# A seven-product scheme (Strassen) for the second matrix product of the last two tiles

## The chip, the cores and the metric

The kernel runs on one core of one Trainium2 chip. A core has five engines that run side by side, each through its own list of instructions in order, and that wait for each other through semaphores: TensorE (PE), which multiplies matrices out of SBUF into PSUM; VectorE (DVE) and ScalarE (ACT), which work on SBUF and PSUM; GpSimd (POOL), which works on SBUF and issues transfers; and SyncE (SP), which issues transfers. The metric is the time of the whole program on the device, in microseconds (us), as the median of three runs.

## The reference, cut to what matters

```python
def _attn_ref(q, k, v):                       # q, k, v: 8 x 8 x 576 x 64 (batch, head, position, 64)
    scores = scale * np.matmul(q, k.transpose(0, 1, 3, 2))
    mask = (rel >= 0) & (rel < 64)            # rel: own position less the key's
    scores = np.where(mask, scores, -1e9)
    attn = softmax(scores)                    # over the keys
    return np.matmul(attn, v)

x = attention output, batch and position as 4608 rows, heads side by side as 512 columns
h = x @ w_in                                  # 512 x 2048
g = h * np.cos(h)
return g @ w_out                              # 2048 x 512
```

Each of the 4608 rows of the attention's output goes through two matrix products with a gate between them. `x @ w_in` is the first product, `g @ w_out` the second.

## The kernel before, in words

The 4608 rows are cut into nine tiles of 512 rows (`mt` = 0 to 8). For one tile PE makes the first product as 16 column blocks of 128 (`ff`), each from four matmuls of 512 columns that accumulate in one PSUM bank (`first`, L458). As soon as a block is done ACT takes its sine with a shift (the cosine, `sin`, L597) and DVE multiplies (`gT`, L600, bf16). The 16 blocks of `gT` lie in eight buffers of two. The second product then has four groups of 128 rows (`ms`); each accumulates 16 matmuls of 512 columns, with `gT` as the loaded weights and `w_out_sb` as the moving operand, into one bank (L611). A copy (DVE or ACT, L121) brings the bank to `out_sb`, and SP stores it (`store`, L478). In the last tile the last 128 rows are made in two column parts of 384 and 128 (`last_rows`, L470), so that the last copy and transfer are small.

The attention of batch `b` is made beside the products of earlier tiles: loads of q, k and v by POOL (L166, L172), scores on PE (L289, L311), maximum and mask on DVE (L326), exponent on ACT (L338), reciprocal on DVE (L348), the product with it on POOL (`w`, L355), the turn of `w` by a transfer that SP issues, copies of parts of v on POOL (`spread_v`, L121), and the product with v on PE (`values`, L390), which `put_x` copies into `xT`, the input of the next tile's first product. The last batch, 7, is worked on in tile 6; the value products of tile 8 are made inside the second product of tile 7.

The order on each engine is written out in the program. Tile 0 follows the list `FIRST`. From tile 1 on a plan holds steps with due times in units of which a tile has `T` = 32: `at(time, fn, ...)` enters a step, and `pump(time)`, called after each block of the first product and after each quarter of a group of the second, issues all steps that are due. The due times set only the order of instructions; an engine runs ahead of them where its waits allow.

PSUM has eight banks. Three rotate under one tag (`ps_t`), the other five have names: `O1`, `X0`, `X1`, `S`, `O0`. The first product's blocks go round them in this order (`H_BANKS`), and begin with the blocks 0, 1, 2 (`SKEW` = 3) side by side, in `O1`, `X0`, `X1`. The second product uses `O1` and `O0`. SBUF buffers rotate too: `out_sb` has three, `sin` four.

Of the kernel before, what the change touches and what calls it, by code (L numbers as in the profile page):

```python
# [14 lines left out]
F32 = mybir.dt.float32  # L15
BF16 = mybir.dt.bfloat16
AF = mybir.ActivationFunctionType
ALU = mybir.AluOpType
# [14 lines left out]
Q = 16  # L33
T = 2 * Q
# [3 lines left out]
OUTS = 3  # L38
FILL = (6, 12)
TURNED = {4: 2, 5: 2, 6: 2, 7: 6}  # L40

# [23 lines left out]
def kernel(  # L67
# [9 lines left out]
    nc = tc.nc  # L77
# [3 lines left out]
    d_model = H * D  # L81
    d_ff = moe_w_in.shape[1]
    n_ff = d_ff // 128
    MT = 512
    TU = MT // 64
    n_mt = B * S // MT

    ctx.enter_context(tc.manual_schedule())
    const = ctx.enter_context(tc.tile_pool(name="const", bufs=1))
    ld = ctx.enter_context(tc.tile_pool(name="ld", bufs=2))  # L90
    att = ctx.enter_context(tc.tile_pool(name="att", bufs=3))
    moe = ctx.enter_context(tc.tile_pool(name="moe", bufs=2))
# [6 lines left out]
    w_out_sb = const.tile([128, n_ff, d_model], BF16, name="w_out")  # L99
# [4 lines left out]
    mask16 = const.tile([128, 6, 128], BF16, name="mask16")  # L104

    small = const.tile([128, 1], F32, name="small")

    st = {}

# [5 lines left out]
    half = MT // 2  # L115

    def bank(which, name):
        return ps.tile([128, 512], F32, tag=which, name=name)

    def copy(engine, out, in_):  # L120
        {"a": nc.scalar.copy, "p": nc.gpsimd.tensor_copy}.get(engine, nc.vector.tensor_copy)(out, in_)  # L121
# [20 lines left out]
    def rows_tile(name):  # L142
        return ld.tile([128, NC * H * D], BF16, tag=name, name=name)
# [49 lines left out]
    def transposed(name, b, p):  # L193
# [7 lines left out]
        else:  # L201
            for c in range(TURNED.get(b, 0) if name == "q" else 0, NC):
                nc.tensor.transpose(t_ps[:, NP * c:NP * c + NP], of[:, c, 128 * p:128 * p + 128], ident[:NP, :NP])  # L203
# [9 lines left out]
    def put_q(b, p, engine=None):  # L213
        if b > 1:
            lo = TURNED.get(b, 0) * NP
            copy(engine, qsets[b % 2][:, p, lo:], st.pop(("tq", b, p))[:, lo:])
# [232 lines left out]
    def exp_table():  # L449
        nc.scalar.activation(small, small, AF.Exp, scale=0.0)  # L450
# [4 lines left out]
    def first(mt, ff, ks, start, stop):  # L455
        if start:
            st["h", ff] = bank(H_BANKS[mt == 1][ff], "h_ps")
        nc.tensor.matmul(out=st["h", ff], lhsT=w_in_sb[:, ks, ff * 128:ff * 128 + 128],  # L458
                         rhs=st["xT", mt][:, ks], start=start, stop=stop)

    def skewed(mt, ks, n):
        for ff in range(SKEW):
            first(mt, ff, ks, n == 0, n == PAIRS - 1)

    def last_rows(gT, o_sb):
        ms = MT // 128 - 1
        for which, lo, hi in (("O0", 0, LAST), ("S", LAST, d_model)):
            o_ps = bank(which, "out_ps")[:, lo:hi]
            for ff in range(n_ff):
                nc.tensor.matmul(out=o_ps, lhsT=gT[ff // 2][:, ff % 2, ms * 128:ms * 128 + 128],  # L470
                                 rhs=w_out_sb[:, ff, lo:hi], start=ff == 0, stop=ff == n_ff - 1)
            to = moe.tile([128, MT], F32, tag="sin", name="last_sb", bufs=4)[:, lo:hi] if lo else o_sb[:, 1, lo:hi]
            copy("d" if lo else "a", to, o_ps)
            (nc.sync if lo else nc.scalar).dma_start(out=out[n_mt * MT - 128:n_mt * MT, lo:hi], in_=to)

    def store(o_sb, mt, ms0, e, n):
        r0 = mt * MT + (ms0 + e) * 128
        nc.sync.dma_start(out=out[r0:r0 + n * 128].rearrange("(a p) f -> p a f", p=128), in_=o_sb[:, e:e + n])  # L478

    plan = []  # L480

    def at(time, fn, *args):
        plan.append((time, len(plan), fn, args))

    def pump(time):
        plan.sort(key=lambda x: x[:2])
        while plan and plan[0][0] <= time:
            _, _, fn, args = plan.pop(0)
            fn(*args)
# [20 lines left out]
    for b in range(2, B):  # L510
        t0 = T * (b - 1)
        for c in range(TURNED.get(b, 0)):
            at(t0 - T + (24.3 if b == 4 else 23.4 if c < 2 else 26.4) + 0.01 * c, turn_q, b, c)
        for p in range(PAIRS if TURNED.get(b) != NC else 0):
            t_q = t0 + (2 if b == 2 else 1) + (3.3 if b == 2 else 3.5) * p
# [8 lines left out]
        for c in range(5):  # L524
            at(t0 + (8 if TURNED.get(b) == NC else 0.5) + c, load_v, b, c)
        for half_ in range(2):
# [13 lines left out]
            at(time + (0.2 if p < 2 else 0.2 + 0.1 * p), put_x, mt, p, "a" if p == 2 else None)  # L540


    for i in (2, 1):
        at(T + 4 - 0.1 * i, g_trans, n_listed - i)

# [35 lines left out]
    for mt in range(1, n_mt):  # L581
        base = mt * T
        gT = []
        for ks in range(PAIRS):
            pump(max([base - 1] + [time for time, _, fn, args in plan if fn is put_x and args[:2] == (mt, ks)]))
            skewed(mt, ks, ks)
        for ff in range(n_ff):
            for ks in range(PAIRS):
                if ff >= SKEW:
                    first(mt, ff, ks, ks == 0, ks == PAIRS - 1)  # L590
            h_ps = st.pop(("h", ff))
            sin = moe.tile([128, MT], F32, tag="sin", name="sin", bufs=4)
            if ff % 2 == 0:
                gt = moe.tile([128, 2, MT], BF16, tag="gT", name="gT", bufs=n_ff // 2 + 2)
                gT.append(gt)
            e = ff % 2
            nc.scalar.activation(sin, h_ps, AF.Sin, bias=math.pi / 2.0)  # L597
            if ff == n_ff - 1 and mt < B - 1:
                exp_table()
            nc.vector.tensor_tensor(out=gt[:, e], in0=h_ps, in1=sin, op=ALU.mult)  # L600
            pump(base + ff)
        for ms0 in range(0, MT // 128, 2):
            o_sb = moe.tile([128, 2, d_model], F32, tag="out", name="out_sb", bufs=OUTS)
            o_ps = [bank(which, "out_ps") for which in (("O1",) if mt == n_mt - 1 and ms0 else ("O1", "O0"))]
            for e in range(2):
                ms = ms0 + e
                if mt == n_mt - 1 and ms == MT // 128 - 1:
                    last_rows(gT, o_sb)
                    break
                for ff in range(n_ff):  # L610
                    nc.tensor.matmul(out=o_ps[e], lhsT=gT[ff // 2][:, ff % 2, ms * 128:ms * 128 + 128],  # L611
                                     rhs=w_out_sb[:, ff], start=ff == 0, stop=ff == n_ff - 1)
                    if ff % 4 == 3:
                        if ff == n_ff - 1:
                            copy("a" if e and (mt > 1 or ms0) else "d", o_sb[:, e], o_ps[e])
                            if mt == n_mt - 1:
                                store(o_sb, mt, ms0, e, 1)
                        pump(base + Q + 4 * ms0 + (e * n_ff + ff) // 4)
            if mt < n_mt - 1:
                at(base + T + 0.5 + ms0 / 2, store, o_sb, mt, ms0, 0, 2)  # L620
# [30 lines left out]
```

## Time and profile before

| what | value |
|---|---|
| median of three runs | 306.56 us (305.95 to 306.98) |
| span of the profiled execution | 304.8 us |
| PE busy in it | 293.2 us, 96% |
| DVE, ACT, POOL busy | 217.4, 233.7, 195.8 us |

The profile gives the profiled execution's own time as its span, from the first to the last instruction; the median of the runs is 1.76 us above it, which is what lies around the span. In the profile's lines L12 is line 12 of the kernel; a group's row has its operation, what it writes and reads with the shapes, how often it ran, its busy time and the mean time of one, and how long its engine was idle ahead of it and for whom. Rows of a timeline begin with the start and the length in us. A matmul's length in the rows holds its way through the array; the rate at which matmuls follow each other is read from their starts.

### The profile page before, as it was taken

The page shows a single profiled execution, that of the slowest core. Times are in us where ns is not written, and L with a number is a line of the kernel's source. Part 1 is how long each engine was busy: PE and PEld are TensorE (multiplying, and loading weights), DVE is VectorE, ACT ScalarE, POOL GpSimd, SP SyncE. Part 2 cuts the span into 40 slices and gives each one's busy share as a digit, 9 for nine tenths or more (in the row PEclk, how much of TensorE's full clock was granted, in tenths as well). Part 3 has the DMA queues.
Part 4 walks back from the last instruction along what each step waited for, and adds up shares of the span by engine and source line. Part 5 has one row for each costly group of instructions (what it writes and reads, how often), then busy time and mean ns, then how long its engine had stood idle before and what let it go on. Part 6 is the DMA issues. An engine that isn't in the chain of part 4 may idle for free.

```text
span 304.8 us, 8261 instructions
## 1 busy us (share of the span) xinstructions
PE 293.2 (96%) x2840; PEld 154.4 (51%) x2840; DVE 217.4 (71%) x868; ACT 233.7 (77%) x783; POOL 195.8 (64%) x226
## 2 busy tenths in 40 slices
PE   3789999999999999999999999999999999999995
PEld 3667854644455445444544444444544454454443
DVE  3797888898888877787678867886778677236701
ACT  5998699878986799779976998699869986116500
POOL 8899568986999579985998599769804930000000
PEclk9999999999999999999999999999999999999999
DMA  7999999999979995999999999999996852011011
GB/s 144 175 203 184 196 189 142 103 132 169 232 115 115 228 147 80 106 153 233 133 116 150 223 138 109 128 235 148 107 123 147 139 120 98 0 71 69 3 69 69
DMA packets 158186, 41.44 MB, mean 136 GB/s; under 512 B 146944, under 2 KB 153408, under 8 KB 158144
## 3 DMA queue, kind: packets, MB, share of 16 engines
q0 software_dynamic: 100192, 18.06, 80.8%
q1 hardware_dynamic: 57808, 22.66, 40.7%
q8 instruction: 22, 0.36, 0.5%
q14 instruction: 20, 0.16, 0.2%
q10 hardware_dynamic: 144, 0.20, 0.2%
HBM read 36.70 MB, written 9.44 MB: 151 GB/s over the span
## 4 chain that ended last, share of the span: by engine, by line
PE 90%; DVE 3%; DMA 2%; POOL 2%; ACT 1%; issue 1%; POOLq 0%
PE h_ps L458 37%; PE out_ps L611 36%; PE out_ps L441 5%; PE h_ps L422 4%; PE s_ps L289 3%; PE o_ps L390 3%; DMA k<-in_k_dram 2%; PE tq_ps L203 1%; PE out_ps L470 1%; DVE negm L321 1%; POOL q L149 1%; PE s_ps L311 1%; POOL k L149 1%; ACT e L338 0%; DVE wT L121 0%
## 5 line engine op out<-in xcount | busy, mean ns | idle before, releaser
L458 PE MATMUL h_ps<-xT,w_in 128*128 128x512 bf16 x512 | 115.1, 379 | 0.2
L611 PE MATMUL out_ps<-w_out,gT 128*128 128x512 bf16 x496 | 110.0, 379 | 0.0
L600 DVE TENSOR_TENSOR gT<-h_ps,sin 128x512 bf16<-128x512 f32 x128 | 85.1, 688 | 29.3 <-ACT sin L597 28.7
L338 ACT ACTIVATE e<-s,negm 128x128 f32<-128x128 f32 (+1 forms) x256 | 97.2, 382 | 1.7 <-POOL v L121 1.0
L597 ACT ACTIVATE sin<-h_ps 128x512 f32<-128x512 f32 x128 | 73.8, 598 | 31.4 <-PE h_ps L458 30.8
L355 POOL TENSOR_TENSOR w<-e,rden 128x512 bf16<-128x512 f32 (+1 forms) x68 | 69.3, 1033 | 30.8 <-DVE rden L348 25.0
L458 PEld LDWEIGHTS <-w_in 128*128 128x128 bf16 x512 | 48.9, 98 | 54.7
L611 PEld LDWEIGHTS <-gT 128*128 128x128 bf16 x496 | 47.4, 98 | 56.1
L326 DVE CUSTOM_DVE_ANT_0 s<-s_ps,mask 128x128 f32<-128x128 f32 (+1 forms) x256 | 56.1, 277 | 1.7 <-PE s_ps L311 1.4
L338 ACT ACTIVATION_READ_ACCUMULATOR e<-s,negm 128x1 f32 x256 | 48.3, 189 | 0.0
L172 POOL DMA_DIRECT2D v<-in_v_dram x40 | 34.1, 870 | 1.0 <-DMA q<-in_q_dram 1.0
L166 POOL DMA_DIRECT2D q<-in_q_dram x36 | 28.7, 797 | 7.6 <-DMA v<-in_v_dram 2.5
L166 POOL DMA_DIRECT2D k<-in_k_dram x36 | 28.5, 792 | 6.4 <-DMA k<-in_k_dram 4.5
L121 ACT COPY out_sb<-out_ps 128x512 f32<-128x512 f32 (+1 forms) x16 | 9.0, 563 | 23.9 <-PE out_ps L611 18.4
L348 DVE RECIPROCAL rden<-den 128x4 f32<-128x4 f32 (+1 forms) x73 | 12.2, 167 | 19.4 <-ACT e L338 19.0
L121 POOL COPY v<-v 64x1536 bf16<-64x1536 bf16 (+3 forms) x16 | 22.9, 1433 | 0.4
L121 DVE COPY out_sb<-out_ps 128x512 f32<-128x512 f32 x20 | 13.7, 687 | 12.1 <-PE out_ps L611 12.0
L121 DVE CAST xT<-o_ps 128x512 bf16<-128x512 f32 x24 | 15.6, 679 | 8.6 <-PE o_ps L390 8.4
L326 DVE DVE_READ_ACCUMULATOR2_ANT negm<- 128x1 f32 x256 | 21.3, 83 | 0.1
L441 PE MATMUL out_ps<-w_out,gT 128*128 128x512 bf16 x64 | 14.8, 380 | 0.0
L422 PE MATMUL h_ps<-xT,w_in 128*128 128x256 bf16 x128 | 14.6, 273 | 0.0
L422 PEld LDWEIGHTS <-w_in 128*128 128x128 bf16 x128 | 12.3, 98 | 1.4
(67 smaller groups left out, 230.9 us busy)
## 6 DMA issues: line engine op xcount, KB each, us to landing
out_dram<-out_sb SPq DMA_DIRECT2D x16, 512.0 KB, 7.3
v<-in_v_dram POOLq DMA_DIRECT2D x32, 128.0 KB, 6.0
q<-in_q_dram POOLq DMA_DIRECT2D x36, 96.0 KB, 8.7
k<-in_k_dram POOLq DMA_DIRECT2D x36, 96.0 KB, 8.6
w_in<-in_moe_w_in_dram POOLq DMA_DIRECT2D x4, 512.0 KB, 9.2
w_out<-in_moe_w_out_dram POOLq DMA_DIRECT2D x4, 512.0 KB, 11.0
q<-in_q_dram POOLq DMA_DIRECT2D x7, 144.0 KB, 6.5
k<-in_k_dram POOLq DMA_DIRECT2D x7, 144.0 KB, 6.7
```

The lines of the kernel that those rows point to most:

```text
L121: {"a": nc.scalar.copy, "p": nc.gpsimd.tensor_copy}.get(engine, nc.vector.tensor_copy)(out, in_)
L166: nc.gpsimd.dma_start(out=st[name, b][:, c].rearrange("p (h d) -> p h d", h=H), in_=src.rearrange("h p d -> p h d"))
L172: nc.gpsimd.dma_start(out=vt.rearrange("p (h d) -> p h d", h=H), in_=v[b, :, c * 128:c * 128 + n, :].rearrange("h p d -> p h d"))
L326: nc.vector.tensor_tensor_reduce(out=s[:, u, c], in0=s_ps[:, u, c], in1=mask[:, 2 - j % 2 if j else 0, c], scale=-scale if b else -1.0, sc ...
L338: nc.scalar.activation(e[:, u, c], s[:, u, c], AF.Exp, bias=negm[:, u:u + 1], scale=1.0 if n < n_first else -1.0, accum_out=den[:, u:u + 1])
L355: (nc.gpsimd if engine == "p" else nc.vector).tensor_tensor(out=w[:, 0:u], in0=e[:, 0:u], op=ALU.mult, in1=rden[:, 0:u].unsqueeze(2).to_br ...
L422: nc.tensor.matmul(out=h_ps[:, half * e:half * e + half], lhsT=w_in_sb[:, ks, ff * 128:ff * 128 + 128], rhs=st["xT", 0][:, ks, half * g:ha ...
L441: nc.tensor.matmul(out=st["out", m], lhsT=st["g", ff // 2][:, ff % 2, m * 128:m * 128 + 128], rhs=w_out_sb[:, ff], start=ff == 0, stop=ff ...
L458: nc.tensor.matmul(out=st["h", ff], lhsT=w_in_sb[:, ks, ff * 128:ff * 128 + 128], rhs=st["xT", mt][:, ks], start=start, stop=stop)
L597: nc.scalar.activation(sin, h_ps, AF.Sin, bias=math.pi / 2.0)
L600: nc.vector.tensor_tensor(out=gt[:, e], in0=h_ps, in1=sin, op=ALU.mult)
L611: nc.tensor.matmul(out=o_ps[e], lhsT=gT[ff // 2][:, ff % 2, ms * 128:ms * 128 + 128], rhs=w_out_sb[:, ff], start=ff == 0, stop=ff == n_ff - 1)
```

## The change

In tiles 7 and 8 (`FAST`) the second product is made by Strassen's scheme in its form with fewer sums. `gT` of the tile is seen as 2 x 2 blocks (256 rows by 1024 of the inner dimension), `w_out` as 2 x 2 blocks (1024 by 256 columns). Seven products of half size, 16 matmuls of 256 columns each, take the place of the 64 matmuls of 512 columns.

- `sum_weights`: four sums of blocks of `w_out`, each in four pieces of 128x512 (bf16): the first two sums in tiles 2 to 5, one piece a tile on POOL and one on DVE; the other two in tile 6, eight pieces on POOL, into the buffers of q and k rows that are free by then.
- `sum_rows`: four sums of blocks of `gT`, 16 operations of 128x512 (bf16) on DVE, behind the tile's last gate.
- `fast_second`: the products in the order P1, P2, P4, P5, P6, P7, P3. Each fills one bank as two halves of 256 columns (`e` = 0, 1: the two groups of 128 rows). P1 and P2 accumulate in the same bank (`X`, at `O1`), P5 and P3 (`Z`, at `X1`), P6 and P7 (`Y`, at `O1` again); P4 has `W`, at `O0`. Between the two of a pair the first is read: `p1` (a copy on ACT) behind P1, `t5` (a copy on ACT) behind P5, `t6` = P6 + `p1` (DVE) behind P6. Behind P7 DVE makes `t67`, then the four halves of two output blocks; behind each half of P3 it makes that half of the last block. In tile 8 each half of an output block, 128x256, is stored by itself; there is no `last_rows` any more.

```diff
+FAST = (7, 8)
+PRODUCTS = ("P1", "P2", "P4", "P5", "P6", "P7", "P3")
...
+    w_sums = const.tile([128, 2, n_ff // 2, MT // 2], BF16, name="w_sums")
...
+    def b_block(k_, j):
+        return w_out_sb[:, n_ff // 2 * k_:n_ff // 2 * k_ + n_ff // 2, half * j:half * j + half]
+
+    def sum_weights(i, f, engine):
+        d = slice(2 * f, 2 * f + 2)
+        if ("T", i) not in st:
+            st["T", i] = w_sums[:, i] if i < 2 else rows_tile("qk"[i - 2])[:, 0:n_ff // 2 * half].rearrange("p (a n) -> p a n", n=half)
+        in0, in1 = ((b_block(0, 1), b_block(0, 0)), (b_block(1, 1), st["T", 0]),
+                    (b_block(1, 1), b_block(0, 1)), (b_block(1, 0), st.get(("T", 1))))[i]
+        (nc.gpsimd if engine == "p" else nc.vector).tensor_tensor(out=st["T", i][:, d], in0=in0[:, d], in1=in1[:, d], op=ALU.subtract)
+
+    def sum_rows(gT):
+        sums = [[att.tile([128, 4, half], BF16, tag="se"[i], name="sums", bufs=6) for i in range(2)] for _ in range(4)]
+        s1, s2, s3, s4 = [[pair[i // 2][:, 2 * (i % 2):2 * (i % 2) + 2] for i in range(4)] for pair in sums]
+        a = [[[gT[f + 4 * k_][:, :, half * i:half * i + half] for f in range(4)] for k_ in range(2)] for i in range(2)]
+        for to, in0, in1, op in ((s1, a[1][0], a[1][1], ALU.add), (s2, s1, a[0][0], ALU.subtract),
+                                 (s3, a[0][0], a[1][0], ALU.subtract), (s4, a[0][1], s2, ALU.subtract)):
+            for f in range(4):
+                nc.vector.tensor_tensor(out=to[f], in0=in0[f], in1=in1[f], op=op)
+        return {"P1": a[0][0], "P2": a[0][1], "P4": a[1][1], "P5": s1, "P6": s2, "P7": s3, "P3": s4}
+
+    def fast_second(mt, gT):
+        lhs = sum_rows(gT)
+        rhs = {"P1": b_block(0, 0), "P2": b_block(1, 0), "P4": st["T", 3], "P5": st["T", 0], "P6": st["T", 1],
+               "P7": st["T", 2], "P3": b_block(1, 1)}
+        to = {"P1": "X", "P2": "X", "P4": "W", "P5": "Z", "P6": "Y", "P7": "Y", "P3": "Z"}
+        at_bank = {"X": "O1", "W": "O0", "Z": "X1", "Y": "O1"}
...
+        def keep(name, where, other=None):
+            temp[name] = moe.tile([128, 2, half], F32, tag="sin", name=name, bufs=4)
+            if other is None:
+                copy("a", temp[name], acc[where])
+            else:
+                nc.vector.tensor_tensor(out=temp[name], in0=acc[where], in1=temp[other], op=ALU.add)
+
+        def result(o_sb, c, of, other=None, e=None):
+            for e in range(2) if e is None else (e,):
+                cols = slice(half * c, half * c + half)
+                in0 = acc[of] if of in acc else temp[of]
+                if other is None:
+                    copy("a", o_sb[:, e, cols], in0[:, e])
+                else:
+                    nc.vector.tensor_tensor(out=o_sb[:, e, cols], in0=in0[:, e], in1=temp[other][:, e], op=ALU.add)
+                if mt == n_mt - 1:
+                    r0 = mt * MT + 128 * e + (half if o_sb is o2 else 0)
+                    nc.sync.dma_start(out=out[r0:r0 + 128, cols], in_=o_sb[:, e, cols])
+
+        def after_p7():
+            keep("t67", "Y", "p1")
+            result(o2, 0, "W", "t67")
+            result(o2, 1, "t67", "t5")
+
+        after = {"P1": lambda: keep("p1", "X"), "P2": lambda: result(o1, 0, "X"), "P5": lambda: keep("t5", "Z"),
+                 "P6": lambda: keep("t6", "Y", "p1"), "P7": after_p7}
+        for n, name in enumerate(PRODUCTS):
...
+            for e in range(2):
+                for f in range(n_ff // 2):
+                    nc.tensor.matmul(out=acc[where][:, e], lhsT=lhs[name][f // 2][:, f % 2, 128 * e:128 * e + 128],
+                                     rhs=rhs[name][:, f], start=new and f + e == 0, stop=f == n_ff // 2 - 1, skip_group_check=True)
+                if name == "P3":
+                    result(o1, 1, "Z", "t6", e)
+                elif e and name in after:
+                    after[name]()
+                pump(mt * T + Q + (2 * n + e + 1) * (T - Q) / (2 * len(PRODUCTS)) - 1)
...
+    for n in range(16):
+        i, f = divmod(n, 4)
+        if i < 2:
+            at(T * (2 + n // 2) + (14.3, 19)[n % 2], sum_weights, i, f, "pv"[n % 2])
+        else:
+            at(T * (FAST[0] - 1) + (5.8 if i == 2 else 9.8) + f, sum_weights, i, f, "p")
...
+        if mt in FAST:
+            fast_second(mt, gT)
+            continue
```

More of the change, by code (lines that the diff above doesn't have):

```diff
@@ new lines, in fast_second @@
+    def fast_second(mt, gT):
[4 more added lines that the diff above has]
+        at_bank = {"X": "O1", "W": "O0", "Z": "X1", "Y": "O1"}
+        acc, temp = {}, {}
+        o1, o2 = (moe.tile([128, 2, d_model], F32, tag="out", name="out_sb", bufs=OUTS) for _ in range(2))
+        def keep(name, where, other=None):
[22 more added lines that the diff above has]
+        for n, name in enumerate(PRODUCTS):
+            where = to[name]
+            new = where not in acc
+            if new:
+                acc[where] = bank(at_bank[where], "out_ps").rearrange("p (e n) -> p e n", e=2)
+            for e in range(2):
[7 more added lines that the diff above has]
+                pump(mt * T + Q + (2 * n + e + 1) * (T - Q) / (2 * len(PRODUCTS)) - 1)
+        if mt < n_mt - 1:
+            for ms0, o_sb in ((0, o1), (2, o2)):
+                at(mt * T + T + 0.5 + ms0 / 2, store, o_sb, mt, ms0, 0, 2)
```

## The prediction

> **What bounds the kernel now.** I read the page's busy shares and slices first, then the chain that ended last, then TensorE's (PE's) timeline over the last two tiles, which are the ones whose second product is replaced.
>
> ```profile
> span 304.8 us, 8261 instructions
> ...
> PE 293.2 (96%) x2840; PEld 154.4 (51%) x2840; DVE 217.4 (71%) x868; ACT 233.7 (77%) x783; POOL 195.8 (64%) x226
> ...
> PE   3789999999999999999999999999999999999995
> ...
> POOL 8899568986999579985998599769804930000000
> PEclk9999999999999999999999999999999999999999
> ```
>
> PE is busy 96% of 304.8 us, at the full granted clock in every slice, so a time follows from PE's matmuls plus PE's stops. POOL is empty from slice 34 on, and VectorE (DVE) thins out there: the last two tiles have no attention work beside them. The chain over those tiles (start us, length us, what) says the same:
>
> ```profile
> 258.87 7.77 PE out_ps L611 x36
> 266.64 1.13 PE o_ps L390 x64
> ...
> 273.92 13.81 PE h_ps L458 x64
> 287.73 10.36 PE out_ps L611 x48
> 298.09 3.51 PE out_ps L470 x32
> 301.60 0.02 issue
> 301.62 0.29 DVE last_sb L121
> ```
>
> Nothing but PE stands on it up to the last copy: no matmul there waits for anything. The timeline gives the rates, start to start (start us, length us, engine, line):
>
> ```profile
> 258.70 7.93 PE L611 MATMUL out_ps<-w_out,gT 128*128 128x512 bf16 x36
> ...
> 273.76 13.98 PE L458 MATMUL h_ps<-xT,w_in 128*128 128x512 bf16 x64
> 287.57 10.52 PE L611 MATMUL out_ps<-w_out,gT 128*128 128x512 bf16 x48
> 297.93 3.66 PE L470 MATMUL out_ps<-w_out,gT 128*128 128x384 bf16 x32
> ...
> 29.77 8.46 PE L422 MATMUL h_ps<-xT,w_in 128*128 128x256 bf16 x76
> 38.16 0.47 PE L200 MATMUL tk_ps<-ident,k 64*64 64x64 bf16 x18
> ```
>
> Tile 8 (mt = 8): 48 matmuls of 512 columns from 287.57 to 297.93, 10.36 us, 215.8 ns each; a second product of 64 is 13.81 us. With 256 columns: 76 from 29.77 to 38.16, 8.39 us, 110.4 ns each (one weight load per matmul, as in the new product).
>
> **The change: what PE gains.** Seven products of 16 matmuls at 110.4 ns are 7 x 1.77 = 12.36 us, against 13.81: 1.45 us less per tile, 2.9 us for tiles 7 and 8. This is the whole gain, if PE never stops.
>
> **What PE now waits for.** The products P1, P2, P4, P5, P6, P7, P3 share accumulators: P2 accumulates on P1's bank after ScalarE (ACT) has copied P1 out (p1), P7 on P6's after DVE has formed t6, P3 on P5's after t5. In the changed kernel's instruction order the first matmul of P2 waits for the ACT copy p1, the first of P7 for the DVE sum t6, and the ninth of P3 (its second half, e = 1) for the DVE sum that reads P3's first half, as both lie in bank X1. P3's wait for t5 is over long before. PE runs in order, and the next product stands right behind, so nothing covers these three stops. The hand-over times:
>
> ```profile
> 291.22 0.69 DVE L121 COPY out_sb<-out_ps 128x512 f32<-128x512 f32 x1 [2.13 <-PE out_ps L611]
> ...
> 4.41 0.67 ACT L121 CAST k<-rows 128x576 bf16<-128x576 f32 x1 [0.21 <-DMA rows<-in_k_dram]
> 5.13 0.69 PE L200 MATMUL tk_ps<-ident,k 64*64 64x64 bf16 x18 [0.19 <-ACT k L121]
> ...
> L121 ACT COPY out_sb<-out_ps 128x512 f32<-128x512 f32 x15 | 8.5, 569 | 18.4 <-PE out_ps L611 18.4
> ...
> L600 DVE TENSOR_TENSOR gT<-h_ps,sin 128x512 bf16<-128x512 f32 x128 | 85.1, 688 | 29.3 <-ACT sin L597 28.7
> L326 DVE CUSTOM_DVE_ANT_0 s<-s_ps,mask 128x128 f32<-128x128 f32 x228 | 52.6, 284 | 0.7 <-PE s_ps L311 0.4 <-PE s_ps L289 0.3
> L326 DVE CUSTOM_DVE_ANT_0 s<-s_ps,mask 128x64 f32<-128x64 f32 x28 | 5.2, 217 | 1.0 <-PE s_ps L311 1.0
> L131 DVE TENSOR_TENSOR mask<-mask 128x128 f32<-128x128 f32 x1 | 0.3, 293 | 1.0 <-POOL mask L127 1.0
> ```
>
> The sixteenth matmul's slot ends at 287.57 + 16 x 0.2158 = 291.02 and the copy behind it starts at 291.22: 0.20 us from PE to a reader. The cast of k ends at 5.08 and PE starts at 5.13: 0.05 us back. The ACT copy of 128x512 is 0.57 us. A DVE sum of 128x512 out of PSUM is 0.69 us. One of 128x256 isn't in the trace: 284 ns for 128 elements and 217 for 64 make 1.05 ns an element, so 0.42 us (between 0.28 and 0.69); from SBUF alone 293 ns for 128, so 0.43.
>
> With P1's start at 0, one tile runs so: P1 to 1.77; p1 from 1.97 to 2.54; P2 from 2.59 to 4.36 (stop 0.82); P4 to 6.13; P5 to 7.90; P6 to 9.67; t6 from 9.87 to 10.56; P7 from 10.61 to 12.38 (stop 0.94). P3's first half ends at 13.26. DVE meanwhile has, ahead of that half's sum, t67 (12.58 to 13.27) and the four sums of the other two output blocks (0.42, 0.42, 0.43, 0.43, to 14.97). So the sum of the first half ends at 15.39, P3's second half runs from 15.44 to 16.32 (stop 2.18) and its sum from 16.52 to 16.94. The three stops are 3.94 us against 1.45 gained: PE leaves the tile 16.32 - 13.81 = 2.51 us later.
>
> A page speaks against this layout: the Trainium skill's "PSUM — Partial Sum Buffer", section "PSUM bank collisions raise a hardware error", says that two engines at one bank and quadrant at once are an error even at different columns, and wants waits per bank. No row of this trace shows it. By that rule the 2.18 us stop can't be dropped while both halves share a bank.
>
> **Tile 7 to tile 8.** The third matmul of tile 8's first product (ff = 2, bank X1) waits for P3's last sum: it could start at 16.32 + 0.43 = 16.75 and starts at 16.99. That is 0.24 us more, 2.75 for tile 7. The value matmuls (64, 1.13 us in the chain) stand between P5 and P6 now and inside the product before, so they cost the same.
>
> **The end.**
>
> ```profile
> 301.62 0.29 DVE L121 COPY last_sb<-out_ps 128x128 f32<-128x128 f32 x1 [2.80 <-PE out_ps L470]
> 301.94 0.33 SPq L474 DMA_DIRECT2D out_dram<-last_sb  x1
> ...
> out_dram<-out_sb SPq DMA_DIRECT2D x3, 256.0 KB, 2.0
> out_dram<-last_sb SPq DMA_DIRECT2D x1, 64.0 KB, 1.6
> ```
>
> Before, the last copy ends at 301.91, which is 14.34 us after 287.57. Now the last sum ends 16.94 after P1's start: 2.60 us later. The last transfer is 128 KB where it was 64 KB; 64 KB take 1.6 us to land and 256 KB 2.0, so 0.15 more. The eight output transfers on SP's queue need 0.33 us each to issue, and the four before the last pair are issued by the time their sums end (14.97), so SP is free.
>
> **Sums of rows.** Sixteen DVE operations of 128x512, all bf16 in SBUF, enter DVE's queue behind the last gate; t6 stands behind all of them, and in tile 7 behind three xT copies too. The trace has no bf16 sum. Rows to both sides:
>
> ```profile
> L121 DVE COPY wT<-tw_ps 128x512 bf16<-128x512 bf16 x11 | 4.4, 410 | 1.7 <-PE tw_ps L371 1.6
> L121 DVE CAST xT<-o_ps 128x512 bf16<-128x512 f32 x24 | 15.6, 679 | 8.6 <-PE o_ps L390 8.4 <-PE o_ps L408 0.2
> ...
> 288.40 0.69 DVE L600 TENSOR_TENSOR gT<-h_ps,sin 128x512 bf16<-128x512 f32 x1 [0.17 <-ACT sin L597]
> ```
>
> The f32 sum is 0.69 us (L600), the bf16 copy of the same size 0.41, where an f32 copy (291.22 above) takes 0.69. I take 0.41, as these operands are 16-bit on all sides. The last gate ends at 289.09, 1.52 us after the product began; 16 x 0.41 = 6.6 takes DVE to 8.1, before t6 is due at 9.87, and s1 is there (3.2) when P5 begins (6.13). In tile 7 the three xT copies follow the value matmuls and end about 9.9, t6 being due at 11.00. So the sums cost nothing up to 0.52 us apiece in tile 8. Cover gone: at 0.69 they end at 12.56, t6 is 2.69 late in tile 8 and 12.56 + 3 x 0.68 - 11.00 = 3.6 in tile 7, together 6.3.
>
> The Trainium skill's "VectorE: DVE Perf Modes" ("What auto-detection actually checks") says a two-tensor sum takes the double rate when every tensor is 16-bit with unit step; from its side-by-side table (a fixed 158 cycles at 0.96 GHz) I estimate 0.43 us, so no loss here. By the L600 row alone the sum would be 6.3 us higher.
>
> **Sums of weights.** Twelve pieces on POOL, four on DVE, each 128x512.
>
> ```profile
> 216.07 4.28 POOL L172 DMA_DIRECT2D v<-in_v_dram  x5
> 232.24 1.04 POOL L355 TENSOR_TENSOR w<-e,rden 128x512 bf16<-128x512 f32 x1 [11.89 <-DVE rden L348]
> ...
> 237.78 3.41 POOL L121 COPY v<-v 64x1536 bf16<-64x1536 bf16 x2
> ...
> 107.15 0.78 POOL L166 DMA_DIRECT2D k<-in_k_dram  x1
> 108.22 1.03 POOL L355 TENSOR_TENSOR w<-e,rden 128x512 bf16<-128x512 f32 x1 [0.29 <-DVE rden L348]
> ...
> v<-in_v_dram POOLq DMA_DIRECT2D x32, 128.0 KB, 6.0
> ...
> L355 POOL TENSOR_TENSOR w<-e,rden 128x512 bf16<-128x512 f32 x65 | 66.9, 1042 | 30.3 <-DVE rden L348 25.0 <-issue 2.0 <-POOL w L355 1.7
> ```
>
> POOL's nearest operation is 1.04 us. Eight pieces lie in tile 6 among the v loads, where POOL idles 11.89 us after them: 8.3 us fit, with 3.6 over, though seven of them (7.3 us) go ahead of the last v load, which was issued at about 219.5 and would land 6.0 us after 226.8, at 232.8, ahead of the copies at 237.78. One POOL piece in each of tiles 2 to 5 stands ahead of the last k load and of the softmax products; in tile 3 the next of those moves by about 0.75 (0.29 idle taken up) and the gaps behind it (about 0.5 each) give it back. The DVE pieces (0.41) stand behind an output copy, ahead of a memset and a reciprocal, for which POOL waits; PE reads none of these within that tile. I take 0; the other end is all eight of tiles 2 to 5 on the path, 4 x 1.04 + 4 x 0.41 = 5.8.
>
> **Sum.** 2.75 + 2.60 + 0.15 + 0 = 5.5 us: the span goes from 304.8 to 310.3. The median of the runs shown, 306.56, lies 1.76 above the span, which I keep: 312.0 us.
>
> **Rivals.**
> - It gets faster: the readers keep up, so that P2, P7 and P3's second half find their wait done. For it speaks that DVE and ACT are nearly idle there; against it that each reader needs the whole product just ended. It decides in its favour only when the three stops together fall below 1.45 us, from 3.94. With none: 306.56 - 2.9 + 0.13 + 0.15 + 0 = 303.9 us.
> - P3's second half doesn't wait: then P3 ends at 14.15, its last sum at 15.81; tile 7 costs 0.34 + 1.28 (bank X1 free at 15.86 instead of 14.58), tile 8 1.47, with 0.15 in all 3.2: 309.8 us.
> - The row sums run at L600's 0.69: 312.0 + 6.3 = 318.3 us.
> - The weight pieces delay the attention of tiles 2 to 5: up to 5.8, so 312 to 317.8 us; the idle gaps in POOL's rows speak against it.
>
> **How the numbers follow.** The forecast 0.70 (its own range 310.4 to 315.1: five 128x256 sums stand in each tile's chain ahead of P3's second half and one behind, so 0.28 apiece takes 6 x 2 x 0.14 = 1.7 off and 0.69 adds 6 x 2 x 0.26 = 3.1); P3 without wait 0.06; slow row sums 0.09; weight pieces 0.08; faster 0.05; 0.02 that losses and gain cancel. Under 0.3% (0.9 us) a measurement can't tell from no change. So faster 0.05, same 0.02, slower 0.93. The range from 309.0 to 316.0 holds the forecast, the case without P3's wait and most of the weight pieces, some 0.83.
>
> **What would show it.** In the changed profile: 16 matmuls at 110 ns start to start; in each of the two tiles one stop of PE for ACT (about 0.8 us) and two for DVE (about 0.9 and 2.2); h_ps in tile 8 waiting about 0.2 for DVE; row sums near 0.41; no new wait of PE in tiles 2 to 6; POOL's idle in tile 6 down to about 3.6. I'm wrong if PE doesn't stop behind P1, P6 and the half of P3, or if row sums are above 0.5 us.

## The result, and the profile after

The changed kernel takes 311.1 us (median of 4 runs, 310.58 to 312.22), the kernel before 306.75 us in the same comparison: a ratio of 1.0139, 95% interval 1.0109 to 1.0169. It is slower, by some 4.3 us, as forecast (312.0, range 309.0 to 316.0). Its profiled execution has a span of 308.8 us and a time of 310.58 us. Of all the runs reported below one, of 309.18 us in the fourth experiment, took over 1.5% longer than the fastest of its kernel and is left out of that ratio.

The page's first rows:

```profile
span 308.8 us, 8467 instructions
...
PE 288.0 (93%) x2889; PEld 162.4 (53%) x2920; DVE 232.9 (75%) x915; ACT 234.6 (76%) x787; POOL 209.0 (68%) x238
...
PEclk9999999999999999999999999999999999999998
```

PE is busy 5.2 us less than before and the span is 4.0 us longer: matmuls were saved, and stops took their place. Not all of the 5.2 is saved work: this trace has 2889 matmuls for 2920 weight loads, so 31 matmuls have no record, while the one before has 2840 of each. The fifth experiment's trace, with 2920 of each and no stops, has PE busy for 290.7 us, 2.5 less than before. Whom PE waited for, from the profile's view of waits (us in total, times, longest us):

```profile
PE out_ps L546 <- DVE out_sb L527: 3.4, 2, 1.7
...
PE out_ps L546 <- DVE t L518: 1.7, 2, 0.9
...
PE out_ps L546 <- ACT p L124: 1.4, 2, 0.7
...
PE h_ps L461 <- DVE out_sb L527: 0.3, 1, 0.3
```

L546 is the line of the seven products. PE waits twice each, once a tile, for `p1`, for `t6`, and for the sum of P3's first half; and once for bank X1 at the start of tile 8. PE's timeline of tile 7 shows where (start us, length us, what, and in brackets the idle time before):

```profile
257.95 1.91 PE L546 MATMUL out_ps<-w_out,gT 128*128 128x256 bf16 x16
260.54 1.91 PE L546 MATMUL out_ps<-w_out,gT 128*128 128x256 bf16 x16 [0.68 <-ACT p L124]
262.28 1.91 PE L546 MATMUL out_ps<-k,gT 128*128 128x256 bf16 x16
264.03 1.91 PE L546 MATMUL out_ps<-w_sums,sums 128*128 128x256 bf16 x16
265.87 1.20 PE L393 MATMUL o_ps<-wT,v 128*64 128x64 bf16 x64
267.00 1.92 PE L546 MATMUL out_ps<-w_sums,sums 128*128 128x256 bf16 x16
269.77 1.91 PE L546 MATMUL out_ps<-q,sums 128*128 128x256 bf16 x16 [0.85 <-DVE t L518]
271.52 1.04 PE L546 MATMUL out_ps<-w_out,sums 128*128 128x256 bf16 x8
274.25 1.03 PE L546 MATMUL out_ps<-w_out,sums 128*128 128x256 bf16 x8 [1.70 <-DVE out_sb L527]
275.12 0.38 PE L461 MATMUL h_ps<-xT,w_in 128*128 128x512 bf16 x1
275.80 13.54 PE L461 MATMUL h_ps<-xT,w_in 128*128 128x512 bf16 x61 [0.30 <-DVE out_sb L527]
```

P2 starts at 260.54 and P4, which waits for nothing, at 262.28: 1.74 us a product, 109 ns a matmul. Against that the stops are, from the end of a product's last slot, 260.54 - 259.69 = 0.85 us behind P1, 269.77 - 268.75 = 1.02 behind P6, and 274.25 - 272.39 = 1.86 in the middle of P3. (The brackets show about 0.17 less, as the row of a product, 1.91 us, is that much longer than its 1.74.) The two tiles by their ends:

| stretch | before | after | difference | predicted |
|---|---|---|---|---|
| tile 7, second product with values | 258.70 to 273.76: 15.06 | 257.95 to 275.12: 17.17 | +2.11 | +2.51 |
| tile 8, first product | to 287.57: 13.81 | to 289.18: 14.06 | +0.25 | +0.24 |
| tile 8, to the end of DVE's last operation | to 301.91: 14.34 | to 305.74: 16.56 | +2.22 | +2.60 |
| from there to the end of the span | 2.89 | 3.06 | +0.17 | +0.15 |
| sum | | | +4.75 | +5.5 |

The span grew by 4.0 only, as this execution reached tile 7 0.75 us earlier. That was so already in tile 0, where the block of 96 matmuls of the first product starts at 26.81 instead of 27.58, ahead of every changed instruction; from there to tile 7 the two executions take 231.14 and 231.12 us. The changed tiles are therefore compared by their own stretches here.

### The profile page after: what moved, and what is told of

It is laid out like the page before. It is cut to its first block, busy times and chain, and to the rows that moved or that the text cites. A ratio compares the mean times of both kernels' runs of the same rounds, so it can differ in the third digit from the quotient of the medians.

```text
span 308.8 us, 8467 instructions
## 1 busy us (share of the span) xinstructions
PE 288.0 (93%) x2889; PEld 162.4 (53%) x2920; DVE 232.9 (75%) x915; ACT 234.6 (76%) x787; POOL 209.0 (68%) x238
## 4 chain that ended last, share of the span: by engine, by line
PE 87%; POOL 4%; DVE 3%; issue 2%; DMA 2%; ACT 0%; DVEq 0%; POOLq 0%
PE h_ps L461 36%; PE out_ps L698 27%; PE out_ps L546 8%; PE h_ps L425 5%; PE out_ps L444 4%; PE s_ps L292 3%; PE o_ps L393 3%; DMA q<-in_q_dram 2%; PE tq_ps L206 1%; POOL w L358 1%; DVE out_sb L527 1%; POOL v L175 1%; DVE t L518 1%; PE tw_ps L374 1%; PE s_ps L314 1%
## 5 line engine op out<-in xcount | busy, mean ns | idle before, releaser
L681 ACT ACTIVATE sin<-h_ps 128x512 f32<-128x512 f32 x128 | 73.8, 598 | 40.1 <-PE h_ps L461 38.6
L698 PE MATMUL out_ps<-w_out,gT 128*128 128x512 bf16 x372 | 82.9, 379 | 1.7 <-issue 1.6
L698 PEld LDWEIGHTS <-gT 128*128 128x128 bf16 x384 | 36.5, 98 | 43.1
L351 DVE RECIPROCAL rden<-den 128x4 f32<-128x4 f32 (+1 forms) x73 | 12.2, 167 | 18.4 <-ACT e L341 18.1
L546 PEld LDWEIGHTS <-sums 128*128 128x128 bf16 x128 | 12.4, 98 | 7.2 <-issue 5.8
L444 PE MATMUL out_ps<-w_out,gT 128*128 128x512 bf16 x60 | 14.3, 379 | 0.3 <-issue 0.2
L431 ACT ACTIVATE sin<-h_ps 128x512 f32<-128x512 f32 x16 | 9.2, 596 | 3.3 <-PE h_ps L425 3.3
```

The source lines that it names most:

```text
L546: nc.tensor.matmul(out=acc[where][:, e], lhsT=lhs[name][f // 2][:, f % 2, 128 * e:128 * e + 128], rhs=rhs[name][:, f], start=new and f + e ...
```

## Experiments

All times are medians beside runs of the kernel before on the same chip. In the first four those runs have a median of 306.88 us (29 runs, 305.53 to 308.86), in the last three 306.8 (11 runs).

**P3 in one piece.** The wait inside P3 alone is taken away: both sums that read it stand behind its second half.

```diff
-                if name == "P3":
-                    result(o1, 1, "Z", "t6", e)
+                if e and name == "P3":
+                    result(o1, 1, "Z", "t6")
```

> Edit: both sums that read P3 stand behind its second half, so that this half waits for nothing. Theory (three stops of PE per tile, 0.85, 1.02 and 1.86 us in the changed kernel's trace): the 1.86 us stop goes; DVE's queue behind P7 (t67 0.69, four sums 1.5, two sums 0.8) then ends 3.2 us behind P7 instead of 4.2, so bank X1 comes free and the last sum ends about 1.0 earlier in each tile: 309.0 us, with a new wait of tile 8's third matmul of about 1.1 us. Rival (the loss lies elsewhere, in the weight pieces or the 256-column matmuls): 311.1 us, no change.

Measured: 309.76 us (4 runs), ratio 1.0112 (1.0069 to 1.0155). PE's waits, and the border of the tiles in its timeline:

```profile
PE out_ps L546 <- DVE t L518: 1.7, 2, 0.9
...
PE h_ps L461 <- DVE out_sb L527: 0.9, 1, 0.9
```

```profile
272.61 1.91 PE L546 MATMUL out_ps<-w_out,sums 128*128 128x256 bf16 x16
274.36 0.38 PE L461 MATMUL h_ps<-xT,w_in 128*128 128x512 bf16 x1
275.68 13.54 PE L461 MATMUL h_ps<-xT,w_in 128*128 128x512 bf16 x61 [0.94 <-DVE out_sb L527]
```

DVE's last two sums in tile 8, and SP's issues of that tile's eight output transfers (count; shortest, median, longest ns; first and last start):

```profile
303.65 0.75 DVE L527 TENSOR_TENSOR out_sb<-out_ps,t 128x256 f32<-128x256 f32 x2
```

```profile
L530 SPq DMA_DIRECT2D out_dram<-out_sb x8: 332/395/403, 294.0 to 305.1; - x8
```

P3 runs through (272.61 to 274.36, 1.75 us), but the third matmul of tile 8 (one of the two ahead of it has no record) now waits 0.94 us by its bracket where it waited 0.30: bank X1 is read by the last sum, which DVE reaches behind t67 and five others. Tile 7 falls from 17.17 to 15.31, tile 8's first product rises from 14.06 to 14.70, tile 8's second falls from 16.56 to 15.34: 2.44 us less up to the last sum, where about 2.1 (311.1 to 309.0) was expected for the whole. But the span now ends 3.90 us behind that sum (304.40 to 308.3), where it was 3.06, and SP starts its last issue some 0.7 us behind the sum, where it was 0.03. So 1.6 us are left, and the medians say 1.3. The intervals of the two ratios overlap; what this edit does is read from the rows. Removing the stop gave back a third of it at tile 8's start (0.64 of 1.86), since the queue of DVE was behind it, and at the program's end another 0.84.

**Another order of products.** The third stop stays; the first two get another product in between.

```diff
-PRODUCTS = ("P1", "P2", "P4", "P5", "P6", "P7", "P3")
+PRODUCTS = ("P1", "P4", "P5", "P6", "P2", "P7", "P3")
...
-        at_bank = {"X": "O1", "W": "O0", "Z": "X1", "Y": "O1"}
+        at_bank = {"X": "O1", "W": "O0", "Z": "X1", "Y": "X0"}
```

> Edit: products in the order P1, P4, P5, P6, P2, P7, P3 (P6's bank X0 in place of O1), so that another product stands between P1 and P2 and between P6 and P7. Theory: the stops of 0.85 and 1.02 us go in both tiles, the third stays: 311.1 - 2 x 1.87 = 307.4 us. Rival (the row sums on DVE aren't ready so early, or the stops only move): P6 waits for DVE and the time stays above 309.5 us.

Measured: 307.79 us (10 runs), ratio 1.0038 (1.0015 to 1.0062). Of the products' waits PE has one kind left, 1.7 us in each tile:

```profile
PE out_ps L546 <- DVE out_sb L527: 3.4, 2, 1.7
```

Tile 7 takes 15.32 us (259.95 to 275.27), 1.85 less than in the changed kernel, for stops of 0.85 and 1.02. P6 starts 5.2 us behind P1 there and doesn't wait for the row sums. The third stop is as long as before, which fits with its being DVE's queue and nothing that the order of the others changes.

**The pieces of weight sums alone.** In the kernel before, the sixteen pieces are made and nothing reads them.

```diff
+    w_sums = const.tile([128, 2, n_ff // 2, MT // 2], BF16, name="w_sums")
...
+    def sum_weights(i, f, engine):
...
+    for n in range(16):
...
```

> Edit: the kernel before with the sixteen pieces of weight sums alone, which nothing reads; the second product is the old one. Theory: they lie in idle time of POOL and DVE: 306.75 us, within 0.9. Rival (the pieces are part of the loss): up to 4 x 1.17 + 4 x 0.42 = 6.4 us more; or, since tile 7 began 0.75 us earlier in the changed kernel's trace, 306.0 us.

Measured: 306.48 us (10 runs), ratio 0.9987 (0.9963 to 1.0012): no difference that these runs can tell; by the interval the pieces cost at most 0.4 us of the 4.3. The second rival's 306.0 lies inside the interval, but the 0.75 us need no such reason: the start of tile 0's block of 96 matmuls, ahead of every changed instruction, lies between 26.43 and 28.05 us in the nine traces, here at 27.91. This profiled execution does take 232.95 us from that block to tile 7, with two waits of PE for a transfer of `wT` ahead of tile 4's first product (1.5 us in all in the view of waits); the first two experiments take 231.79 and 231.90, the changed kernel, the kernel before and the next experiment 231.1, the last three 231.74 to 232.01. A wait for `wT`, of 0.3 to 0.4 us, also stands in the traces of the first, second and fifth experiments, all of which have the pieces, and in none of the other five, of which four have them. Whether the pieces make such a delay more frequent, one trace of each kernel can't show; over ten runs it leaves no trace in the median.

**All three stops taken away.** The order of the second experiment, P3 in one piece as in the first, the two sums of t67 and t5 on POOL, so that they don't stand ahead of P3's sums in DVE's queue, and P4's bank exchanged for that of P5 and P3. (The diff shows the banks and the move to POOL; the rest is as above.)

```diff
-        at_bank = {"X": "O1", "W": "O0", "Z": "X1", "Y": "O1"}
+        at_bank = {"X": "O1", "W": "X1", "Z": "O0", "Y": "X0"}
...
-                    nc.vector.tensor_tensor(out=o_sb[:, e, cols], in0=in0[:, e], in1=temp[other][:, e], op=ALU.add)
+                    (nc.vector if of in acc else nc.gpsimd).tensor_tensor(out=o_sb[:, e, cols], in0=in0[:, e], in1=temp[other][:, e], op=ALU.add)
```

> Edit: the order of products of the run before last, both sums of P3 behind its second half and ahead of the sums of t67 and t5, which go to POOL; P4 in X1, P5 and P3 in O0. Theory: no stop of PE is left; tile 7 saves 13.81 - 12.2 = 1.6 us; in tile 8 the last sum ends 13.2 us behind P1's start where the old last copy ended 14.34 behind it, 1.1 less; the last transfers cost 0.2: 306.75 - 2.5 = 304.2 us. Rival (Strassen's seven products don't pay here at all): 306.7 us or more.

Measured: 305.71 us (12 runs, 11 of them from 303.69 to 306.62), ratio 0.9953 (0.9927 to 0.9978): faster than the kernel before, by less than expected. PE's timeline from tile 7's second product to the start of tile 8; then DVE's last sums and SP's issues of the eight output transfers in tile 8:

```profile
257.64 1.91 PE L546 MATMUL out_ps<-w_out,gT 128*128 128x256 bf16 x16
259.39 1.91 PE L546 MATMUL out_ps<-k,gT 128*128 128x256 bf16 x16
261.13 3.66 PE L546 MATMUL out_ps<-w_sums,sums 128*128 128x256 bf16 x32
264.72 1.20 PE L393 MATMUL o_ps<-wT,v 128*64 128x64 bf16 x64
265.85 1.92 PE L546 MATMUL out_ps<-w_out,gT 128*128 128x256 bf16 x16
267.61 1.91 PE L546 MATMUL out_ps<-q,sums 128*128 128x256 bf16 x16
269.36 1.91 PE L546 MATMUL out_ps<-w_out,sums 128*128 128x256 bf16 x16
271.10 13.98 PE L461 MATMUL h_ps<-xT,w_in 128*128 128x512 bf16 x62
```

```profile
297.40 0.76 DVE L527 TENSOR_TENSOR out_sb<-out_ps,t 128x256 f32<-128x256 f32 x2 [0.32 <-issue]
```

```profile
L530 SPq DMA_DIRECT2D out_dram<-out_sb x8: 332/396/1094, 294.2 to 299.2; - x8
```

No bracket is left on PE in either tile. Tile 7 is 13.46 us (257.64 to 271.10) against 15.06 before, 1.60 less, and tile 8 ends its last sum 13.24 us behind P1 against 14.34, 1.10 less: both as expected. What is missing is the end: the last sum is done at 298.16 and the span ends at 302.3, 4.14 us later where it was 2.89. Four of the transfers become ready in little more than a microsecond, and SP starts the last issue at 299.2. So tile 8 as a whole gains nothing: 1.10 on the products, 1.25 lost behind them. The stretches make 1.60 + 1.10 - 1.25 = 1.45 us, and the ratio of 0.9953 makes 1.44.

**The transfers on two queues.**

```diff
-                    nc.sync.dma_start(out=out[r0:r0 + 128, cols], in_=o_sb[:, e, cols])
+                    queue = nc.scalar if of == "t67" or (of == "Z" and e) else nc.sync
+                    queue.dma_start(out=out[r0:r0 + 128, cols], in_=o_sb[:, e, cols])
```

> Edit: as e4_all_stops, but in tile 8 the transfers of the block t67 + t5 and of P3's second half are issued by ACT, which is idle, and not by SP. In e4_all_stops the last sum ends at 298.16 and the span at 302.3, 4.14 us later, where the kernel before has 2.89 and the changed kernel 3.06; SP's last issue starts at 299.2, 1.07 behind the sum. Theory: SP's queue of issues makes the tail, and it falls by about 1.0: 304.7 us. Rival (the 512 KB themselves take that long to write): no change, 305.7 us.

Measured: 305.38 us (6 runs), ratio 0.9958 (0.9931 to 0.9985). ACT's three issues and the last sum, then the transfers (issues, KB each, median us to landing):

```profile
299.28 1.54 ACTq L531 DMA_DIRECT2D out_dram<-out_sb  x3
299.50 0.76 DVE L527 TENSOR_TENSOR out_sb<-out_ps,t 128x256 f32<-128x256 f32 x2 [0.32 <-issue]
```

```profile
out_dram<-out_sb SPq DMA_DIRECT2D x5, 128.0 KB, 2.1
out_dram<-out_sb ACTq DMA_DIRECT2D x3, 128.0 KB, 2.2
```

The span ends 3.74 us behind the last sum (300.26 to 304.0): 0.4 of the 1.25 lost come back, not 1.0, and the medians don't tell the two apart. The wait for the queue is all but gone: the last issue, ACT's third, starts at 300.4 (its row of 0.4 us ends at 300.82), 0.2 us behind the last sum, where it was 1.0. But the span ends 3.6 us behind that issue, where it was 3.1, so half of what was won there is lost again. Landing takes 2.1 to 2.2 us here where it took 1.8 in the run before, which would fit several transfers under way at once; that was not tried by itself, and the rival, that the bytes take that long, isn't excluded for what is left.

**Tile 7 alone, without stops.** `FAST = (7,)` in the fourth experiment's kernel; tile 8 keeps the old second product and its small last transfer.

> Edit: as e4_all_stops, in tile 7 alone; tile 8 as in the kernel before. Theory: with no stop of PE tile 7 saves 1.6 us (15.06 to 13.46 in e4_all_stops) and nothing else moves: 306.9 - 1.6 = 305.3 us. Rival (what PE saves in tile 7 is given back, as tile 8's first product waits for its input or for a bank): 306.9 us.

Measured: 304.68 us (6 runs, 304.15 to 305.29), ratio 0.9941 (0.9915 to 0.9967), the lowest median of all, though its interval overlaps those of the two runs before. Tile 7 takes 13.46 us again (258.60 to 272.06), and tile 8's first product 13.82, as before: nothing is given back.

**Tile 7 alone, with the stops.** `FAST = (7,)` in the changed kernel.

> Edit: the changed kernel's scheme in tile 7 alone; tile 8 as in the kernel before. Theory: tile 7 costs 2.11 us and the wait for bank X1 0.25: 306.9 + 2.4 = 309.3 us. Rival (the loss is at the program's end): 306.9 us.

Measured: 308.19 us (4 runs), ratio 1.0066 (1.0031 to 1.01).

```profile
PE out_ps L546 <- DVE out_sb L527: 1.7, 1, 1.7
PE out_ps L546 <- DVE t L518: 0.9, 1, 0.9
...
PE out_ps L546 <- ACT p L124: 0.7, 1, 0.7
```

Each wait stands there once. The tile is 17.17 us long (258.17 to 275.34), as in the changed kernel, and tile 8's first product 14.06: the tile's price is 2.36 us by its stretches and 0.95 to 3.1 by the ratio's interval.

## Why the prediction was right

- **The stops behind P1 and P6.** Predicted 0.82 and 0.94, measured 0.85 and 1.02. The copy `p1` took 0.59 instead of 0.57, and `t6` starts 0.28 us behind P6's last slot where `t67`, which waits for PE alone, starts 0.20 behind P7's. The second experiment removes 1.85 of their 1.87.
- **The stop inside P3.** It is where the prediction put it and for the reason given, DVE's queue: in tile 8 these are DVE's rows from `t6` to the last sum.

```profile
299.02 0.69 DVE L518 TENSOR_TENSOR t<-out_ps,p 128x512 f32<-128x512 f32 x1 [2.96 <-PE out_ps L546]
301.71 0.69 DVE L518 TENSOR_TENSOR t<-out_ps,p 128x512 f32<-128x512 f32 x1 [2.00 <-PE out_ps L546]
302.44 0.76 DVE L527 TENSOR_TENSOR out_sb<-out_ps,t 128x256 f32<-128x256 f32 x2
303.11 0.75 DVE L527 TENSOR_TENSOR out_sb<-t,t 128x256 f32<-128x256 f32 x2
303.78 0.42 DVE L527 TENSOR_TENSOR out_sb<-out_ps,t 128x256 f32<-128x256 f32 x1
304.25 1.03 PE L546 MATMUL out_ps<-w_out,sums 128*128 128x256 bf16 x8 [1.70 <-DVE out_sb L527]
305.32 0.42 DVE L527 TENSOR_TENSOR out_sb<-out_ps,t 128x256 f32<-128x256 f32 x1 [1.12 <-PE out_ps L546]
```

  A 128x256 sum takes 0.42 us, as estimated, but two in a row take 0.75 to 0.76, not 0.84 to 0.86: the next one starts before the row of the last one ends. Four such overlaps make the stop 1.86 instead of 2.18. This is the largest mis-sized term of the sum. The first experiment shows the second half of P3 running at once when its reader is moved.
- **The gain.** 1.74 us a product instead of 1.77, so seven take 12.2, and 1.6 us are saved a tile, not 1.45. The fourth experiment shows the whole of it once nothing stops PE. With the stop inside P3 (0.32) this (0.15) makes the predicted loss 0.47 us a tile too high, and the stops behind P1 and P6 make it 0.11 too low. That is 0.36 of the 0.40 by which tile 7 came out better: the errors partly cancelled.
- **Tile 7 to 8, and the end.** 0.25 and 0.17, predicted 0.24 and 0.15. SP's queue of issues was free in the changed kernel, as said: it starts the last one at 305.77, behind the sum that ends at 305.74. An issue took 0.33 to 0.41 us there, not 0.33. In the first and fourth experiments, where the same transfers fall due closer together, the queue isn't free.
- **Sums of rows.** The groups of the first and third of the four row sums and of the last four pieces of the weight sums; then DVE's rows of the first and last row sum in tile 7; then POOL's idle time behind the pieces in tile 6:

```profile
L501 DVE TENSOR_TENSOR sums<-gT 128x512 bf16<-128x512 bf16 x16 | 5.7, 416 | 0.0
L492 POOL TENSOR_TENSOR k<-w_out,w_sums 128x512 bf16<-128x512 bf16 x4 | 4.7, 1170 | 0.1
```

```profile
259.39 1.42 DVE L501 TENSOR_TENSOR sums<-gT 128x512 bf16<-128x512 bf16 x4
...
263.41 1.42 DVE L501 TENSOR_TENSOR sums<-gT,sums 128x512 bf16<-128x512 bf16 x4
```

```profile
231.47 1.04 POOL L358 TENSOR_TENSOR w<-e,rden 128x512 bf16<-128x512 f32 x1 [2.74 <-DVE rden L351]
```

  416 ns a sum (0.41 taken), 0.34 us from one start to the next, so the sixteen are done at 264.83, 6.9 us behind P1's start and 4.2 ahead of `t6`. The rival in which a sum takes L600's 0.69 us is out. The estimate of 0.43 from the Trainium skill's page "VectorE: DVE Perf Modes" agrees with the 416 ns.
- **Sums of weights.** A piece costs POOL 1.17 us, not 1.04, and POOL's idle in tile 6 is 2.74 instead of the 3.6 predicted; the third experiment shows no price on the program (at most 0.4 us by its interval). In the changed kernel's trace PE has no new wait in tiles 2 to 6, as predicted.
- **The rivals.** That P3's second half doesn't wait would have shown no 1.70 in the waits. The faster one needed the three stops below what was gained: they were 3.73 against 1.6. For P3 without its wait the rival's 309.8 is near the first experiment's 309.76, but in part by luck: up to the last sum that run lost 2.14 us where the rival has 3.09, and at the end 1.01 where it has 0.15.

How little of the loss belongs to the scheme, the experiments show: a different order of the same products, other banks and a sum moved turn +1.4% into -0.5%, and in tile 7 alone into -0.6%. The prediction priced the case without stops at 303.9 us, with 0.15 us more for the end. The fourth experiment is that case and takes 305.71; most of what is missing is its end, which is 1.25 us longer than before.

## What to carry to other kernels

Before PE's work is cut into pieces that accumulate on each other, list for each pair what has to be read between the two, and place at least one other piece there: a product of 1.74 us covered a hand-over of 0.85 to 1.02 us fully here. The reader issued per half bought nothing here, where both halves lie in one bank: it made the second half wait for all that stood ahead of the reader in its engine's queue. That two banks would have spared the wait was not tried. In the last tile the gain has also to get past the final transfers: 1.1 us won on PE stood against 1.25 lost where four transfers fell due together, so the scheme paid in tile 7 and not in tile 8.

## What was not expected of the hardware

- POOL takes 1.17 us for a 128x512 sum with bf16 on all sides, more than the 1.04 for its product with f32 inputs: smaller inputs alone didn't make it faster, though the two also differ in the operation and in a broadcast operand. The same sum takes DVE 0.42.
- In the fourth experiment SP starts the last six issues from 296.78 to 299.2, 0.48 us apart on the mean, though the row of one is 0.33 to 0.40 us long. Issuing three of the eight from ACT brought the last issue to 0.2 us behind the last sum but gave back only 0.4 us of the tail; why the end then comes 3.6 us behind that issue, where it was 3.1, stays open.
- `t6`, whose wait names PE and ACT, started 0.27 to 0.28 us behind PE's last slot in the changed kernel, `t67`, which names PE alone, 0.20. No run separates the cause.
